# Weight rounding around the Fourier products of the second batch: one pause in place of two

## The chip, the cores and the metric

The kernel runs on one core of a Trainium2 chip. The metric is the device time of one execution in microseconds (us), and the number compared is the median over several runs. A profile is one execution seen by the hardware profiler; its times count from the first instruction. Its engine names are used throughout: PE is TensorE (PEld its weight loads), DVE is VectorE, ACT is ScalarE, POOL is GpSimd and SP is SyncE, which here only issues DMAs.

## The reference

Eight batches of 576 tokens go through chunked attention (8 heads of 64, chunks of 64 tokens), then through a block that adds the real part of a two-dimensional Fourier transform, normalises, and runs a two-layer MLP with a residual:

```python
scores = scale * np.matmul(q_c, k_c.transpose(0, 1, 2, 4, 3))   # in chunks of 64
attn = softmax(scores)                                          # shortened here
x = (attn @ v_c), heads joined: (8, 576, 512)
mixed = np.real(fft(fft(x, axis=1), axis=2))
u = x + mixed
un = (u - mean(u)) / sqrt(var(u) + 1e-6)
out = u + maximum(un @ w_ch1, 0) @ w_ch2      # w_ch1: 512 x 2048, w_ch2: 2048 x 512
```

The two weight matrices come in 64-bit floating point and must be rounded to 32 bits on the chip. All products are in fp32.

## The kernel before, in words

**Groups and tiles.** The tokens are cut into tiles of 128 rows. `groups` are sets of four tiles that pass the MLP together; group 0 is the first batch, group 1 the second, and so on, and the 64 tokens left over in each batch ("rest" tiles) form a group at the end. `mlp(g)` is a Python generator that issues group g's products and yields after each step: 16 steps for the first layer, then 16 for the second (`down_plain`, line L1095, for group 0). So steps 1 to 16 are group 0's first layer and steps 17 to 32 its second; step 17 + m handles row block m. Each engine has its own queue and takes its instructions from it in the order in which the program lists them, and so does SP with the DMAs that it issues. Engines meet only through semaphores.

**Side work.** Beside `mlp(g)` the driver issues the attention and the Fourier transform of the next batch, `side(b)`, also a generator. For batch 1 it has 26 steps: 17 of attention, three empty ones (PAUSE), and six of `fourier(1)`. The driver spreads them over steps 4 to 25. The attention's steps fall so that attention's last step is issued in step 18, the empty ones in steps 19 and 20, and `fourier(1)` begins in step 21.

**`fourier(b)`** (printed below) makes the token transform in two halves: `z_sets(.., 0)` for the first (L669, and the one-row products L679), then the rest and `z_sets(.., 1)` for the second. ScalarE copies results out (L708, L694), VectorE joins them (`z_joined`, L699, L703), ScalarE writes them in transform order to `zr` and `zf` (L720 to L738). Then each of three `mixed` tiles follows (rest tile first, L788 on TensorE): ScalarE copies half of it (L793, L794), VectorE forms both signs (L798, L799) and adds them to x (L805; the mirrored tiles on POOL), then takes mean and variance (L652, L653), whose inverse root ScalarE forms (L656, L657). The mixing tiles use two PSUM buffers in turn. `normed` (L942 on ScalarE) and `turned` (four PE transposes, L347) later make group 1's operand from them: the first of these is issued with step 26 and step 28.

**Rounding.** The weights are cut into 32 pieces of 128x512. `round_weight(i)` issues the head of piece i (two VectorE instructions, L322 and L325, and three on ScalarE, L314, L317, L320) and the tail of piece i - 1 (three on VectorE, L335, L336, L337), which needs the ScalarE results of that piece. After the tail it issues the load of a further piece (L299, on SP). The driver calls it through `round_next`, once or twice a step, unless a side step of this step was marked heavy:

```python
while done < due:
    heavy = next(sides[cur], None) or heavy
    done += 1
...
if not heavy:
    round_next()
    if t <= 2 or t < KF and t % 4 == 0 or t >= KF + 3:      # KF = 16
        round_next()
if n_w > len(pieces) and t >= KF + 7:
    for _ in range(3):
        next(conv2, None)
```

A generator's yielded value belongs to the work issued ahead of that yield. `n_w` counts the roundings; the value 33 is reached when all are issued.

**After the rounding.** `conv2` runs `keep2(i)` for i = 0 to 3: four VectorE subtractions (L1017) that form combined blocks of w_ch2 in `yall` (i even) or `xall` (i odd), one per driver call, then seven stores of 256 KB to the DRAM buffer s2, issued on SP (L1021), then the next i. `conv1` does the same for w_ch1 on POOL (L999, L1003) from step 32 on. They share SP's queue with the loads of q and k (L203) and v (L226) for the coming attention tiles, and with the output stores (L977 and half of L986; the other half of L986 leaves from ACT's queue). For batch 2 and later, VectorE transposes q and k (L366) just before a tile's scores (L398), and a tile's q or k buffer is loaded again right after that.

Of the kernel before, what the change touches and what calls it, by code (L numbers as in the profile page):

```python
# [16 lines left out]
def kernel(  # L17
# [130 lines left out]
    def kind(n):  # L148
        return tiles[n][0]

    def xt(n):
        return xall[:, place[n], 0:DM + 1]
# [494 lines left out]
    def means(ns):  # L647
        st = sm_p.tile([128, 2, 2], FP32, tag="st", bufs=6 + NP, name="st")
        rstd = sm_p.tile([128, 2], FP32, tag="rstd", bufs=6 + NP, name="rstd")
        for j, n in enumerate(ns):  # L650
            bst = sm_p.tile([128, 6], FP32, tag="bst", name="bst")
            nc.vector.bn_stats(bst, xt(n)[:, 1:DM + 1] if kind(n) == HI else xt(n)[:, 0:DM])  # L652
            nc.vector.bn_aggr(st[:, j], bst)  # L653
            sts[n] = st[:, j, 0:1], rstd[:, j:j + 1]
        g = slice(0, len(ns))
        nc.scalar.activation(out=rstd[:, g], in_=st[:, g, 1], func=ACTF.Ln, bias=eps)  # L656
        nc.scalar.activation(out=rstd[:, g], in_=rstd[:, g], func=ACTF.Exp, scale=-0.5)  # L657
# [3 lines left out]
    def z_sets(z, pm, i, turn_, first=False):  # L661


        for s in range(2):
            for q_ in range(4):
                k, r = (q_ // 2 + turn_) % 2, q_ % 2
                T, p = 2 * k + s, slice(32 * q_, 32 * q_ + 32)
                d0_ = T * HQ if i < NM else s * HQ
                nc.tensor.matmul(  # L669
                    out=z[r][k][:, s * NE:(s + 1) * NE], lhsT=pm[i][p, d0_:d0_ + HQ],  # L670
                    rhs=tk[p, NM - 1 - i if i < NM else NM, k],
                    start=first and s == 0, stop=False, skip_group_check=True,
                )

    def mid_products(outs, pm, i):
        p, m0 = (slice(0, 128), DM) if i < NM else (slice(CH, 128), 2 * HQ)
        for g, out_ in enumerate(outs):
            c0, c1 = halves[g % 2]
            nc.tensor.matmul(  # L679
                out=out_[:, 0:c1 - c0], lhsT=pm[i][p, m0 + g // 2:m0 + g // 2 + 1], rhs=tk[p, NM - 1 - i if i < NM else NM, 0, c0:c1],  # L680
                start=False, stop=i == NM, skip_group_check=True,
            )

    def z_space():


        odd = [ps_t.tile([128, 512], FP32, tag="pt", name="z") for _ in range(2)]
        even = ps_a.tile([128, 2, 512], FP32, tag="att", name="more_z")
        zs[1:] = even, odd
        return odd, [even[:, k] for k in range(2)]  # L690

    def z_odd():
        for k in range(2):
            nc.scalar.copy(zs[0][:, 2 * k:2 * k + 2, 1], zs[2][k][:, 0:2 * NE].rearrange("p (t f) -> p t f", t=2))  # L694

    def z_joined():
        even = zs[1][:, :, 0:2 * NE].rearrange("p k (t f) -> p k t f", t=2)
        z4 = zs[0].rearrange("p (k t) r f -> p k t r f", t=2)
        nc.vector.tensor_tensor(out=z4[:, :, :, 0], in0=even, in1=z4[:, :, :, 1], op=ALU.add)  # L699
        for k in range(2):  # L700
            e, o = even[:, k], z4[:, k, :, 1]
            a, b = (e, o) if k == 0 else (o, e)
            nc.vector.tensor_tensor(out=o, in0=a, in1=b, op=ALU.subtract)  # L703

    def z_middle(outs):
        for g, out_ in enumerate(outs):
            c0, c1 = halves[g % 2]
            nc.scalar.copy(middle[:, g // 2, c0:c1], out_[:, 0:c1 - c0])  # L708
# [4 lines left out]
    def z_tile(zf, i):  # L713


        low, high = zs[0][:, :, 0], zs[0][:, :, 1]
        to = zf[:, :, 128 * i:128 * i + 128].rearrange("p t (c r i) -> p t c r i", c=2, r=2)
        if i == 0:
            for c in range(2):
                nc.scalar.copy(to[:, :, c], by_parity(low[:, :, CH * c + CH:CH * c:-1]))  # L720
            return
        n = (2 * CH + CH - NE + 1) // 2
        nc.scalar.copy(to[:, :, 0, :, 0:n], by_parity(high[:, :, NQ - 1 - 3 * CH:NQ - 1 - 3 * CH + 2 * n]))
        nc.scalar.copy(to[:, :, 0, :, n:], by_parity(low[:, :, NE - 1:2 * CH:-1]))
        nc.scalar.copy(to[:, :, 1], by_parity(high[:, :, CH // 2:CH // 2 + CH]))

    def z_rest(h):

        low, high = zs[0][:, :, 0], zs[0][:, :, 1]
        to = zr[:, :, h].rearrange("p t (r i) -> p t r i", r=2)  # L730
        n = CH // 4
        nc.scalar.copy(to[:, :, :, 0:n], by_parity(high[:, :, 2 * n:0:-1]))
        nc.scalar.copy(to[:, :, 1, 0:1], low[:, :, 0:1])
        for t in (0, 2):
            nc.scalar.activation(
                out=to[:, t:t + 2, :, n:], in_=by_parity(high[:, t:t + 2, 0:2 * n]), func=ACTF.Copy, scale=1.0 - t,
            )
        nc.scalar.copy(to[0:1, 2:3, :, n:], by_parity(high[0:1, 2:3, 0:2 * n]))  # L738
# [3 lines left out]
    def fourier(b):  # L742
        h = b % 2
        zf = one_p.tile([128, 4 * NL + 16], FP32, tag="zf", name="zf")
        zf = zf[:, 0:4 * NL].rearrange("p (t f) -> p t f", t=4)
        zs[0] = one_p.tile([128, 8 * NE], FP32, tag="two", name="zs").rearrange("p (t r f) -> p t r f", t=4, r=2)
        pm = [pms.pop((b, i)) for i in range(NM + 1)]


        z = z_space()  # L750
        for i in range(NM + 1):
            z_sets(z, pm, i, 0, i == 0)
        outs = [z[0][0][32 * g:32 * g + 1, 2 * NE:] for g in range(4)]
        for i in range(NM):
            mid_products(outs, pm, i)
        nc.scalar.copy(middle[:, 0, 0:1], outs[0][:, 0:1])
        yield b == 1
        if b == 1:
            yield
        mid_products(outs, pm, NM)  # L760
        for i in range(NM):
            z_sets(z, pm, i, 1)
        z_middle(outs)
        z_odd()
        if b == 1:
            z_joined()
        else:
            yield
            z_joined()
        nc.scalar.copy(zs[0][0:1, 2], middle)  # L770
        if h == 1:
            z_rest(h)
        for i in range(NM):
            z_tile(zf, i)
        if h == 0:
            z_rest(h)
        yield b == 1

        def mixed(i):
            mix = ps_t.tile([128, 512], FP32, tag="pt", name="mix")  # L780
            zt = zr.rearrange("p t h f -> p t (h f)") if i == NM else zf[:, :, 128 * i:128 * (i + 1)]
            for T, (cols, tab) in enumerate((
                (slice(0, HM + 1, 2), ce),
                (slice(1, HM, 2), co),
                (slice(0, DM, 2), cx),
                (slice(HM + 1, DM, 2), so),
            )):
                nc.tensor.matmul(  # L788
                    out=mix[:, cols], lhsT=zt[:, T], rhs=tab,
                    start=(T == 0), stop=(T == 3), skip_group_check=True,  # L790
                )
            y = three_p.tile([128, XW], FP32, tag="y", name="y")
            nc.scalar.copy(y[:, 0:HM + 1], mix[:, 0:HM + 1])  # L793
            nc.scalar.copy(y[:, DM:DM + 1], mix[:, 0:1])  # L794
            return y, mix

        def both(y, mix):
            nc.vector.tensor_tensor(out=y[:, DM - 1:HM:-1], in0=y[:, 1:HM], in1=mix[:, HM + 1:DM], op=ALU.subtract)  # L798
            nc.vector.tensor_tensor(out=y[:, 1:HM], in0=y[:, 1:HM], in1=mix[:, HM + 1:DM], op=ALU.add)  # L799
            return y  # L800

        def added(y, n):
            x, w = xt(n), DM + (kind(n) == HI)
            eng = nc.gpsimd if kind(n) == HI else nc.vector
            eng.tensor_tensor(out=x[:, 0:w], in0=y[:, 0:w], in1=x[:, 0:w], op=ALU.add)  # L805

        for i in ((NM,) if h == 1 else ()) + tuple(range(NM)):
            y = both(*mixed(i))
            ns = [rests[b // 2]] if i == NM else [at[LO, b, i], at[HI, b, i]]
            for n in ns:  # L810
                added(y, n)
            means(ns)
            yield
# [426 lines left out]
    with tc.manual_schedule():  # L1240
# [48 lines left out]
        def side(b):  # L1289
            yield from attention(b)  # L1290
            for _ in range(PAUSE if b == 1 else PAUSE - 1):
                yield
            yield from fourier(b)
# [107 lines left out]
```

## Time and profile before

| What | Value |
|---|---|
| Median of 5 runs | 1091.36 us (1090.13 to 1094.23) |
| The profiled execution's own time | 1091.36 us |
| Its span, first to last instruction | 1089.6 us |
| Granted TensorE clock, mean over the span | 0.994 |
| DMA traffic | 192.65 MB, mean 177 GB/s |
| Instructions | 19740 |

The span lies 1.8 us under the execution's own time, and that execution is at the median. The page's first part gives each engine's busy time and share; its second part cuts the span into 40 slices of 27.2 us. Further answers of the trace are named by what they list: the timeline (instructions of an engine in order of time, with the idle time before one in brackets and what ended it), the waits (who waited for whom in total, times, and the longest), the chain of waits (followed back from the last instruction) and the table by stretches (busy time of PE, PEld, DVE, ACT and POOL, then the granted TensorE clock, the busy share of the DMA engines and their GB/s).

### The profile page before, as it was taken

To read this page: it belongs to the slowest core of one execution; us is meant where nothing else is said; L and a number is where in the kernel's file an instruction comes from. 1 tells how busy PE (TensorE), PEld (TensorE's weight loads), DVE (VectorE), ACT (ScalarE), POOL (GpSimd) and SP (SyncE) were. 2 spreads that over 40 slices of the span, in tenths; PEclk is the share of its full clock that TensorE was granted. 3 is DMA by queue.
4 is the path that set the end of the run, shared out by engine and by line. 5 is a ranking of instruction groups with operands and counts; after the bars stand their busy time and mean duration, and the time that the engine had idled before them with its cause. 6 is when DMAs were issued, how large, how long until landed. Compare 5 with 4: busy or idle time off the path is not lost.

```text
span 1089.6 us, 19740 instructions
## 1 busy us (share of the span) xinstructions
PE 1058.9 (97%) x7410; PEld 841.3 (77%) x7410; DVE 591.1 (54%) x1287; ACT 309.6 (28%) x730; POOL 308.1 (28%) x459
## 2 busy tenths in 40 slices
PE   8999998889999999999999999999999999999998
PEld 6645454335888888888888888888888888888887
DVE  4899979234456555574456555745664534323411
ACT  4788463111202231223023312331134103101300
POOL 4301001356413441163306240535152401220140
PEclk9999999989999999999999999999999999999999
DMA  8776535688556826794568356864653355446232
GB/s 167 227 209 177 154 107 173 193 273 281 197 183 191 246 97 186 209 264 133 169 203 248 106 179 178 253 171 155 192 191 102 140 183 174 125 153 212 78 116 78
DMA packets 147948, 192.65 MB, mean 177 GB/s; under 512 B 66284, under 2 KB 104172, under 8 KB 140686
## 3 DMA queue, kind: packets, MB, share of 16 engines
q1 hardware_dynamic: 144204, 187.98, 56.5%
q10 hardware_dynamic: 3330, 2.76, 1.0%
q8 instruction: 59, 0.97, 0.4%
q0 software_dynamic: 320, 0.66, 0.3%
q14 instruction: 35, 0.29, 0.1%
HBM read 167.22 MB, written 24.12 MB: 176 GB/s over the span
## 4 chain that ended last, share of the span: by engine, by line
PE 82%; DMA 5%; DVE 5%; SPq 3%; ACT 3%; issue 1%; POOL 0%; DVEq 0%; ACTq 0%; POOLq 0%
PE pb L1190 20%; PE pa L1141 17%; PE pa L1190 15%; PE pb L1141 12%; PE up L1074 4%; PE dn L1095 3%; PE pt L347 2%; PE z L669 2%; PE mix L788 2%; PE xp L448 1%; PE sc L398 1%; PE up L1054 1%; DMA v<-in_v_dram 1%; SPq L216 1%; DMA wb<-s 1%
## 5 line engine op out<-in xcount | busy, mean ns | idle before, releaser
L1141 PE MATMUL pa<-unT,wa 128*128 128x256 f32 x672 | 159.9, 381 | 1.2 <-DVE wa L1149 1.2
L1141 PEld LDWEIGHTS pa<-unT,wa 128*128 128x128 f32 x672 | 126.2, 190 | 19.1 <-DVE wa L1149 1.7
L1042 POOL TENSOR_TENSOR h<-h 128x256 f32<-128x256 f32 x64 | 55.0, 866 | 230.5 <-DVE wb L1040 137.5
L1190 PE MATMUL pa<-wb,h 128*128 128x256 f32 x512 | 115.7, 380 | 0.0
L1190 PE MATMUL pb<-wb,h 128*128 128x256 f32 x512 | 114.9, 379 | 0.0
L1141 PE MATMUL pb<-wa 128*128 128x256 f32 x448 | 106.6, 381 | 0.0
L1190 PEld LDWEIGHTS pa<-wb,h 128*128 128x128 f32 x512 | 96.0, 190 | 13.0
L1190 PEld LDWEIGHTS pb<-wb,h 128*128 128x128 f32 x512 | 96.3, 190 | 12.6
L1141 PEld LDWEIGHTS pb<-wa 128*128 128x128 f32 x448 | 84.3, 190 | 11.5
L1147 DVE TENSOR_TENSOR wa<-pb,wa 128x256 f32<-128x256 f32 x56 | 23.8, 425 | 69.1 <-ACT wa L1146 69.1
L1074 PE MATMUL up<-unT,wa 128*128 128x512 f32 x128 | 60.8, 629 | 0.0
L1095 PE MATMUL dn<-wb,h 128*128 128x512 f32 x128 | 57.5, 597 | 2.6 <-ACT h L1065 2.6
L505 POOL COPY xall<-xall 1x512 f32<-1x512 f32 x28 | 17.3, 619 | 149.7 <-DVE xall L465 120.4
L1190 PE MATMUL pb<-wb,yall 128*128 128x256 f32 x256 | 58.2, 381 | 0.0
L1190 PE MATMUL pb<-wb 128*128 128x256 f32 x256 | 57.7, 379 | 0.0
L1190 PE MATMUL pa<-wb,yall 128*128 128x256 f32 x256 | 57.6, 379 | 0.0
L1146 ACT COPY wa<-pa 128x256 f32<-128x256 f32 x56 | 20.9, 372 | 123.5 <-PE pa L1141 87.4
L1141 PE MATMUL pa<-wa 128*128 128x256 f32 x224 | 53.9, 383 | 0.0
L1141 PE MATMUL pb<-unT,wa 128*128 128x256 f32 x224 | 52.9, 379 | 0.0
L1190 PEld LDWEIGHTS pa<-wb,yall 128*128 128x128 f32 x256 | 48.0, 190 | 6.1
L1190 PEld LDWEIGHTS pb<-wb,yall 128*128 128x128 f32 x256 | 47.7, 190 | 6.3
L1190 PEld LDWEIGHTS pb<-wb 128*128 128x128 f32 x256 | 47.6, 190 | 5.9
(265 smaller groups left out, 1756.1 us busy)
## 6 DMA issues: line engine op xcount, KB each, us to landing
wb<-s SPq DMA_DIRECT2D x56, 1024.0 KB
wa<-s SPq DMA_DIRECT2D x196, 256.0 KB
xall<-in_moe_w_ch_dram SPq DMA_DIRECT2D x22, 512.0 KB
q<-in_q_dram SPq DMA_DIRECT2D x96, 112.0 KB
k<-in_k_dram SPq DMA_DIRECT2D x96, 112.0 KB
v<-in_v_dram SPq DMA_DIRECT2D x124, 64.0 KB
yall<-in_moe_w_ch_dram SPq DMA_DIRECT2D x10, 512.0 KB
s<-wb SPq DMA_DIRECT2D x20, 256.0 KB
```

The lines of the kernel that those rows point to most:

```text
L216: eng.dma_start(out=t[p0:p0 + np_], in_=src[b, :, c * CH:c * CH + np_, :].rearrange("h p d -> p h d"))
L347: nc.tensor.transpose(pt[:, j, :], src(j), ident)
L505: nc.gpsimd.tensor_copy(to, from_)
L669: nc.tensor.matmul(out=z[r][k][:, s * NE:(s + 1) * NE], lhsT=pm[i][p, d0_:d0_ + HQ], rhs=tk[p, NM - 1 - i if i < NM else NM, k], start=fir ...
L788: nc.tensor.matmul(out=mix[:, cols], lhsT=zt[:, T], rhs=tab, start=(T == 0), stop=(T == 3), skip_group_check=True,)
L1042: nc.gpsimd.tensor_tensor(out=h1[:, m, hi], in0=h1[:, m, lo], in1=h1[:, m, hi], op=ALU.subtract)
L1074: nc.tensor.matmul(out=up, lhsT=w1[:, kk, m * 128:(m + 1) * 128], rhs=unT[:, kk], start=(kk == 0), stop=(kk == KD - 1),)
L1095: nc.tensor.matmul(out=dn, lhsT=h1[:, m, s * 128:(s + 1) * 128], rhs=w2[:, m, :], start=(m == 0), stop=(m == KF - 1),)
L1141: nc.tensor.matmul(out=dst, lhsT=w[:, kk, r], rhs=rhs[o][:, kk], start=(o in (0, 1) and kk == 0), stop=(kk == 1), skip_group_check=True,)
L1146: nc.scalar.copy(a, dst)
L1147: nc.vector.tensor_tensor(out=b, in0=pbs[r][:, 0], in1=a, op=ALU.add)
L1190: nc.tensor.matmul(out=dst, lhsT=lhs[:, m], rhs=w[:, m], start=(o in (0, 2) and m == 0), stop=(m == HF - 1), skip_group_check=True,)
```

## The change

In `fourier(1)` the first half of the products is no longer marked heavy, the empty step between the halves is, and the second half no longer is. For the other batches the marks were false and stay so. The instructions are the same; only where roundings are issued among them changes.

```diff
         nc.scalar.copy(middle[:, 0, 0:1], outs[0][:, 0:1])
-        yield b == 1
+        yield
         if b == 1:
-            yield
+            yield True
         mid_products(outs, pm, NM)
...
         if h == 0:
             z_rest(h)
-        yield b == 1
+        yield
```

Roundings per driver step, and the value that `n_w` has after the step:

| Step | Side work of batch 1 | Before | After |
|---|---|---|---|
| 20 | two empty steps | 2 (28) | 2 (28) |
| 21 | first half of the products | none (28) | 2 (30) |
| 22 | empty | 2 (30) | none (30) |
| 23 | second half, copies to zr and zf | none (30) | 2 (32) |
| 24 | mixing, rest tile | 2 (32) | 1, tail alone (33) |
| 25 | mixing, two tiles | 1, tail alone (33) | none (33) |

With n_w at 33 a step earlier, `conv2` starts in step 24 instead of 25 and is three calls ahead in each later step.

## The prediction, made before the changed kernel was run

> **What bounds the kernel now.** I read the page first: its engine table and the slices.
>
> ```profile
> PE 1058.9 (97%) x7410; PEld 841.3 (77%) x7410; DVE 591.1 (54%) x1287; ACT 309.6 (28%) x730; POOL 308.1 (28%) x459
> ```
>
> TensorE is busy for 1058.9 of 1089.6 us; 30.7 us are idle. An edit that moves no matrix product can pay only in these, or in time at half clock. The list of waits, for TensorE over the whole span, says where they end:
>
> ```profile
> PE sc L398 <- DVE rd L461: 8.6, 1, 8.6
> PE pt L347 <- ACT un L942: 3.6, 3, 2.0
> PE pt L347 <- ACT ex L424: 2.7, 2, 2.0
> ...
> PE pa L1141 <- DVE wa L1149: 1.2, 2, 0.6
> ```
>
> The largest is one wait. In the timeline (TensorE) it stands at 223.36 us, after two of 2 us:
>
> ```profile
> 171.85 0.66 PE L347 MATMUL pt<-ident,un 128*128 128x128 f32 x4 [2.04 <-ACT un L942]
> 208.36 0.78 PE L347 MATMUL pt<-ident,ex 128*128 128x128 f32 x4 [2.00 <-ACT ex L424]
> 208.93 5.21 PE L1074 MATMUL up<-unT,wa 128*128 128x512 f32 x8
> 223.36 1.13 PE L398 MATMUL sc<-kT,qT 64*64 64x64 f32 x32 [8.60 <-DVE rd L461]
> ```
>
> From 223.4 to the end TensorE waits only 1.2 us more (the row L1141), so a shift of 223.4 shifts the end. What ends the 8.6 us? The wait names L461, but the timeline of VectorE, whose queue is in order, has L461 behind a transpose that waits for a DMA, and the chain of waits goes on into the queue of SP:
>
> ```profile
> 222.22 1.09 DVE L366 STREAM_TRANSPOSE kT<-k 128x512 f32<-128x512 f32 x1 [13.54 <-DMA k<-in_k_dram]
> ```
>
> ```profile
> 205.60 0.62 SPq L977
> 206.22 0.06 issue
> 206.28 8.80 DMA out_dram<-o
> 215.08 0.02 issue
> 215.09 0.34 SPq L203
> ...
> 216.98 5.11 DMA k<-in_k_dram
> ```
>
> So a load of k, issued behind the first output stores, sets TensorE's time at 223.4. The stores' data was ready long before: VectorE's L1108 wrote it from 189.49 to 191.96. They left at 205.60 because SP still had the copies that keep2 writes to s2 (L1021) in front. Why SP was late is in its own waits and timeline:
>
> ```profile
> SPq L1021 <- DMA out_dram<-o: 4.1, 1, 4.1
> ```
>
> ```profile
> 189.51 5.29 SPq L1021 DMA_DIRECT2D s<-yall  x3
> ```
>
> One store of s2 out of yall waited 4.1 us for an output store that ACT's queue had issued at 190.80. The two share no data; I read it as a completion counter that the queues use in turn. After it (194.48) SP issued 18 more DMAs up to 205.60: 0.62 us each. Last, the table by stretches: DMA (the last two columns) stands idle from 152 to 172, just before the copies start.
>
> ```profile
> 152.00:156.00 4.00, 4.00 (x16) 2.27 (x15) 2.10 (x4) 1.76 (x8) 0.00 (x0) 1.00 0.00 0
> 168.00:172.00 4.00, 1.97 (x6) 0.66 (x5) 3.68 (x8) 1.88 (x7) 1.02 (x1) 1.00 0.00 0
> 208.00:212.00 4.00, 3.64 (x8) 1.93 (x9) 0.68 (x1) 1.38 (x3) 2.22 (x2) 0.59 0.23 59
> ```
>
> **The change, part by part.** *The first half moves nothing.* By the counts of the driver, step 21 issues the first half of the products and step 22 nothing. The two roundings of step 22 go to step 21. No other VectorE work lies between, and ACT has only L756 there, ahead of them in both. They keep 141.50 to 147.05, and the last two weight loads that they issue on SP (143.49, 146.44) keep their place: zero, as no queue's order changes.
>
> *The second half moves two roundings past the rest tile's mixing,* from step 24 to the end of step 23. On VectorE they fill a hole: L703 ends at 150.38, L798 waits until 153.79 (3.4 us). Two roundings take 5.2 (156.26 to 161.5). But their six ACT instructions now stand ahead of L793 on ACT. ACT is done with zf at 153.35; the six take about 3.9 back to back (0.53, 0.74 and 0.65 a piece, from their starts at 156.81, 157.33 and 158.07). L798 therefore starts at 157.7, not 153.79, and the rest tile ends at 157.7 + 2.55 = 160.25. No load is left for them to issue; the loads that they read were issued by 146.44, and two such loads that VectorE did wait for had landed 3.5 us after theirs (135.33 to 138.89, 140.89 to 144.44): about 150, ahead of the use at 153.0.
>
> *What follows.* The counter n_w reaches 33 in step 24, not 25, so keep2 starts a step earlier. VectorE in step 24: the last piece's tail, 1.9 (169.88 to 171.78), and three of keep2's subtractions, 1.93 (171.78 to 173.71). The next tile's L798 starts at 164.1 instead of 161.64: 2.5 later, and so do the means and L942. TensorE first meets a mixing tile that waits for its PSUM buffer (L799 of the rest tile ends at 158.85, it ran at 157.42: 1.4), then un at 174.35, a wait of 3.1 in place of 2.04. The 0.67 us wait for ex at 177.04 is swallowed. TensorE is then 2.5 - 0.67 = 1.8 behind.
>
> *The clock.* After the wait of 2.0 at 208.36, the eight matmuls took 5.21 us against 3.60, with a granted clock of 0.59 in 208 to 212: it lost 1.6. After 2.04 at 171.85 nothing was lost. A wait of 3.1 lies above both, so I take 1.7 as its price; bounds 0 and 1.7. TensorE is then 3.5 late near 190.
> [...]
>
> *The DMAs of keep2.* Its first copies can leave at 163 to 167, in the idle stretch; the second seven at 174 to 178, ahead of the q loads rather than behind (181.00 to 185.34); the third at 181 to 185 instead of 188.80 to 196.37. SP is seven DMAs ahead in its order. Two bounds for the first output store:
> - Not held by the counter: q loads at 179.4, then in turn third copies, k, v, fourth copies, q to about 195.8, that is 9.8 earlier than 205.60.
> - Held as before: release at 194.45 + 3.5, less some 1.4 because fewer copies crowd that output store (it took 3.6 us): 196.5. With 18 - 7 = 11 still to issue, less 2 because TensorE is later while SP is not: 9 x 0.62 = 5.6, hence 202.1, 3.5 earlier.
>
> I take the second, being nearest to a row that was seen. The k load lands 16.5 after that store, as now (205.60 to 222.1): 218.6, and sc starts at 219.9 instead of 223.37. TensorE is there at 214.77 + 3.5 - 2.0 (the wait at 208.36 goes, the copies it stood on being done) - 1.6 (its half clock) = 214.7. The long wait becomes 5.2 and the half clock after it stays. Sum: -3.5 us on the profiled execution, whose own time of 1091.36 is also the median: 1087.9.
>
> **The rivals.**
> - *SP is not held.* k lands at 212.3, before TensorE wants it. The gain is then 223.37 - 214.7 = 8.7, and the half clock after the long wait goes (24 matmuls took 12.94; at 3.43 for eight they take 10.3, and sc 1.13 against 0.65): 2.9 to 3.1. About 1079.8. For it: 20 us of idle DMA are put to use. Against: the counter's hold is there now.
> - *Gain eaten.* The hold falls with 12 to 15 issues left: 203.9 to 205.8. The time is then 1089.7 to 1091.6. Also here: a k load set by something that does not move.
> - *Slower.* One mechanism: the shared counter. TensorE's lateness delays ACT's output stores, and SP is held on them with all 18 issues left: 196.5 + 11.1 = 207.6, 2.0 late, and the end with it: 1093.4; with a longer landing some 1 to 2 more. It decides from (205.6 - 196.5) / 0.62 = 15 issues left upward.
>
> **How the numbers follow.** Forecast (held, 9 left, 1086 to 1089.5): 0.42. Not held: 0.20. Eaten: 0.18. Slower: 0.20. About 0.2% (2.2 us) is what a measurement of this kernel can tell from no change. Faster by more takes the first two cases: 0.62; same 0.18; slower 0.20. The range reaches down to the unheld case, 1079.0, and up to the slower one, 1093.5; it leaves out deeper gains and a longer hold. The likeliest case's own range is 1086 to 1089.5.
>
> **What would show it.** VectorE without the hole at 150.4 to 153.8, L322 there; L798 of the rest tile near 157.7; the PSUM wait at a mixing tile and the wait for un near 3 us at 174, followed by half clock; s2 copies in the DMA table at 163 to 167; the first output store of SP at 202; the wait at 208.36 gone and the long one near 5 us. I am wrong if the store leaves at or after 205, if the six ACT instructions do not delay L793, or if TensorE finds a new wait behind 223.

## The result, and the profile after

The changed kernel takes 1089.68 us (median of 35 runs, 1086.95 to 1094.19), the kernel before 1091.86 in the 61 runs beside it: ratio 0.9979, 95% interval [0.9972, 0.9987], a gain of 2.2 us. The forecast was 1087.9 with a range of 1079.0 to 1093.5. The profiled execution took 1087.15 us (span 1085.4), 4.2 less than the one of before, and the medians show 2.2 of that.

The page's engine table of the changed kernel, busy time and share:

```profile
PE 1057.5 (97%) x7410; PEld 841.1 (77%) x7410; DVE 592.7 (55%) x1287; ACT 309.6 (29%) x730; POOL 307.9 (28%) x459
```

TensorE's idle time fell from 30.7 to 27.9 us. Its list of waits, changed kernel (total, times, longest):

```profile
PE sc L398 <- DVE rd L461: 6.9, 1, 6.9
PE pt L347 <- ACT un L942: 4.6, 3, 3.0
...
PE mix L788 <- DVE y L799: 1.1, 1, 1.1
```

The long wait at the scores is 1.7 shorter, the wait for un 1.0 longer, the PSUM wait at the mixing tile is new, and ex (L424) has left the list. VectorE's timeline around the rest tile, changed kernel (start, duration, and the idle time before in brackets):

```profile
149.95 0.42 DVE L322 TENSOR_SCALAR wb<-xall 128x512 uint32<-128x512 uint32 x1
...
155.81 0.69 DVE L337 TENSOR_TENSOR wb<-wb,power 128x512 f32<-128x512 f32 x1
157.28 0.42 DVE L798 TENSOR_TENSOR y<-y,mix 128x255 f32<-128x255 f32 x1 [0.78 <-PE mix L788]
...
161.65 0.68 DVE L1017 TENSOR_TENSOR yall<-wb 128x512 f32<-128x512 f32 x1
...
163.58 0.41 DVE L798 TENSOR_TENSOR y<-y,mix 128x255 f32<-128x255 f32 x1
```

The hole is filled from 149.95 on; the rest tile starts at 157.28 instead of 153.79. The releaser is given as PE, but the ACT timeline shows what was last:

```profile
153.05 0.62 ACT L314 ACTIVATE wb<-wb 128x512 f32<-128x512 uint32 x1
...
156.21 0.72 ACT L320 ACTIVATE power<-power,top 128x512 uint32<-128x512 uint32 x1
156.84 0.35 ACT L793 COPY y<-mix 128x257 f32<-128x257 f32 x1
157.09 0.16 ACT L794 COPY y<-mix 128x1 f32<-128x1 f32 x1
```

ACT's six rounding instructions, from 153.05 on, stand ahead of L793, and L794 ends at 157.25, just before L798 starts. TensorE's timeline at the places named in the prediction, and the table by stretches after the wait for un (the value after the five engines is the granted clock), both of the changed kernel:

```profile
173.78 1.10 PE L347 MATMUL pt<-ident,un 128*128 128x128 f32 x4 [3.01 <-ACT un L942]
174.67 4.88 PE L1095 MATMUL dn<-wb,h 128*128 128x512 f32 x8
...
208.92 0.60 PE L347 MATMUL pt<-ident,ex 128*128 128x128 f32 x4
209.36 3.60 PE L1074 MATMUL up<-unT,wa 128*128 128x512 f32 x8
...
220.51 1.13 PE L398 MATMUL sc<-kT,qT 64*64 64x64 f32 x32 [6.92 <-DVE rd L461]
```

```profile
172.00:176.00 4.00, 2.22 (x6) 1.57 (x7) 3.93 (x7) 3.72 (x12) 0.00 (x0) 0.73 0.70 233
176.00:180.00 4.00, 4.00 (x13) 1.86 (x12) 3.97 (x7) 1.31 (x2) 0.48 (x2) 0.84 0.86 304
```

After 3.01 us of idle the clock was 0.73 and 0.84 (0.50 in 174 to 177), and the next eight matmuls took 4.88 us instead of 3.60. At 208.92 wait and half clock are both gone (1.00 in 208 to 212). Last, SP in the changed kernel: its largest wait for a DMA between 125 and 260 us, the two places in its timeline, and what VectorE waits for:

```profile
SPq L226 <- DMA out_dram<-o: 5.6, 1, 5.6
```

```profile
188.16 8.17 SPq L226 DMA_DIRECT2D v<-in_v_dram  x4
...
202.95 1.20 SPq L977 DMA_DIRECT2D out_dram<-o  x2
```

```profile
219.37 1.08 DVE L366 STREAM_TRANSPOSE kT<-k 128x512 f32<-128x512 f32 x1 [12.69 <-DMA k<-in_k_dram]
```

SP is still held, now at a load of v, until 195.05. The first output store leaves at 202.95 (205.60 before), VectorE's transpose of k starts at 219.37 (222.22), the scores at 220.51 (223.36): 2.85 us earlier. Of the profiled execution's gain, 0.7 more lies in the 24 matmuls behind the wait (12.27 us instead of 12.94) and 0.6 in the waits at L1141 (0.6 instead of 1.2).

### The profile page after: what moved, and what is told of

The parts are those of the page before. It is cut to its first block, busy times and chain, and to the rows that moved or that the text cites. A ratio compares the mean times of both kernels' runs of the same rounds, so it can differ in the third digit from the quotient of the medians.

```text
span 1085.4 us, 19741 instructions
## 1 busy us (share of the span) xinstructions
PE 1057.5 (97%) x7410; PEld 841.1 (77%) x7410; DVE 592.7 (55%) x1287; ACT 309.6 (29%) x730; POOL 307.9 (28%) x459
## 4 chain that ended last, share of the span: by engine, by line
PE 88%; DVE 5%; ACT 3%; DMA 3%; issue 1%; SPq 0%; POOL 0%; ACTq 0%; DVEq 0%; POOLq 0%
PE pb L1190 20%; PE pa L1141 18%; PE pa L1190 15%; PE pb L1141 13%; PE up L1074 4%; PE dn L1095 4%; PE pt L347 3%; PE mix L788 2%; PE z L669 2%; PE sc L398 2%; PE xp L448 2%; PE up L1054 1%; DMA v<-in_v_dram 1%; PE idle L1270 1%; DVE power L336 1%; DMA out_dram<-o 1%
## 5 line engine op out<-in xcount | busy, mean ns | idle before, releaser
L1141 PE MATMUL pa<-unT,wa 128*128 128x256 f32 x672 | 159.9, 381 | 0.6 <-DVE wa L1149 0.6
L1141 PEld LDWEIGHTS pa<-unT,wa 128*128 128x128 f32 x672 | 126.2, 190 | 18.3 <-DVE wa L1149 0.8
L1141 PE MATMUL pb<-wa 128*128 128x256 f32 x448 | 106.6, 381 | 0.0
L1141 PEld LDWEIGHTS pb<-wa 128*128 128x128 f32 x448 | 84.3, 190 | 11.5
L1074 PE MATMUL up<-unT,wa 128*128 128x512 f32 x128 | 58.5, 610 | 0.0
L1141 PE MATMUL pa<-wa 128*128 128x256 f32 x224 | 53.9, 383 | 0.0
L1141 PE MATMUL pb<-unT,wa 128*128 128x256 f32 x224 | 52.9, 379 | 0.0
```

Source lines behind the costliest of these rows:

```text
L1074: nc.tensor.matmul(out=up, lhsT=w1[:, kk, m * 128:(m + 1) * 128], rhs=unT[:, kk], start=(kk == 0), stop=(kk == KD - 1),)
L1141: nc.tensor.matmul(out=dst, lhsT=w[:, kk, r], rhs=rhs[o][:, kk], start=(o in (0, 1) and kk == 0), stop=(kk == 1), skip_group_check=True,)
```

## The experiments

Ratios are against runs of the kernel before in the same batch. Times within a trace shift from one execution to another: the first store to s2, which no edit moves, leaves at 146.82 before, at 146.68 after, and between 146.61 and 149.67 in the others. Where two kernels' times are set against each other below, the difference in that start is taken off, or a length within one trace is used. Theories keep the letters they have in the quoted expectations. "The hold" is the stretch in which SP stands at one DMA until an output store of ACT's queue has landed; issues left at its end are counted with the held DMA.

The first half of the edit moves nothing: in the program built with it alone, every engine has the same instructions in the same order as before, and in that with the second half alone the same as after.

**Which part of the change pays: the moved roundings or the earlier copies?** Two kernels, one with each part.

```diff
 # e1_copies_late, the changed kernel: keep2 from step 25, as before
-if n_w > len(pieces) and t >= KF + 7:
+if n_w > len(pieces) and t >= KF + 9:
 # e2_copies_early, the kernel before: keep2 from step 24
-if n_w > len(pieces) and t >= KF + 7:
+if t >= KF + 8:
```

> The changed kernel, but keep2 starts in step 25 as it did before the change; the roundings stay where the change put them. Theory A (the gain comes from keep2's seven copies standing earlier in SP's queue): the gain goes, SP's order is that of before, the first output store leaves near 205 and the long wait of the scores (L398) is back at 8 to 9 us: 1091 to 1092.5. Theory B (the gain comes from the roundings filling VectorE's hole at 150.4 to 153.8): the gain stays, about 1089.7.

> The kernel before, its roundings where they were, but keep2 starts in step 24 as in the changed kernel. Theory A: the gain is there without the moved roundings, as SP's order is that of the changed kernel; VectorE's three subtractions still stand ahead of the next mixing tile (1.9 us), so TensorE waits about 4 us for un near 174 and then loses 1 to 1.7 us to half clock: 1088 to 1090. Theory B: no gain, 1091.5 to 1093.

e1: 1090.11 us, ratio 0.9978 [0.9965, 0.9991]. e2: 1089.98, ratio 0.9975 [0.9959, 0.9992]. Each part alone gives the whole gain. Theory A, that the earlier copies are what pays, fell with e1, and theory B, that the filled hole is, with e2. The two come there by different ways. In e1 TensorE waits 1.09 for un instead of 2.04, and 0.64 for ex (at 206.95) instead of 0.67 and 2.00, ACT's first output store is issued 1.2 us earlier, and SP is held for 2.8 instead of 4.1. In e2 the wait for un is 3.77 with the clock at 0.65 and 0.50 in 172 to 180; ACT's store is 2.9 later, but only 14 issues are left to SP at the release, not 19.

**Is the hold the limit?** Group 0's four stores that leave from ACT's queue are given to POOL's.

```diff
 # e3_pool_stores, the changed kernel
-eng = nc.scalar if r else nc.sync
+eng = (nc.gpsimd if n in groups[0] else nc.scalar) if r else nc.sync
```

> The changed kernel, with the four output stores of group 0 that left from ACT's queue issued from POOL instead. Theory A with the shared completion counter as the hold: the wait of the v load on an output store (5.6 us) goes, the first output store of SP leaves near 197.5 instead of 202.95, the load of k lands near 214, TensorE's long wait shrinks to 0 to 2 us and the half clock after it goes: 1081 to 1085. Rival C (the hold is the DMA traffic itself, not the counter): SP stands still about as long, 1089 to 1090. POOL issues four DMAs more, which may delay its own conv1 work by some us.

1082.9 us, ratio 0.9908 [0.9888, 0.9929]. SP's timeline, e3:

```profile
179.85 1.88 SPq L203 DMA_DIRECT2D q<-in_q_dram  x4
...
188.36 2.65 SPq L226 DMA_DIRECT2D v<-in_v_dram  x4
...
198.21 1.20 SPq L977 DMA_DIRECT2D out_dram<-o  x2
```

The four loads of v take 2.65 us, not 8.17: the hold is gone with ACT's stores. The instructions' own records name what SP had waited for: the load held in the changed kernel waits for the completion counter of the store that ACT issued at 192.74 (both DMAs name counter 105), and that store landed at 195.04, 0.01 before the load was issued. The scores wait 1.26 us at 215.93, and the clock stays at 1.00 after it.

**Why does k land 16 us behind the first store?** Group 0's mirrored low-tile stores (L977) are written as two stores of 32 rows each, in unmirrored row order, so these rows of the output stand in the wrong places.

```diff
 # e4_forward_rows, the changed kernel, group 0 only
-                nc.sync.dma_start(out=to, in_=o[r0:r0 + CH])
+                if n in groups[0]:
+                    for r in range(2):
+                        nc.sync.dma_start(
+                            out=out[b, t0 + 1 + r:t0 + CH + 1:2, :], in_=o[r0 + ODD * r:r0 + ODD * r + ODD]
+                        )
+                else:
+                    nc.sync.dma_start(out=to, in_=o[r0:r0 + CH])
```

> The changed kernel; group 0's four stores of the low tiles, each one DMA with rows in mirrored order and a slowest dimension of two, are written as two DMAs each of 32 rows in forward order (so these rows of the output stand in the wrong order). Theory D (the load of k lands late because these four stores run on few DMA engines and k's packets queue behind them): SP issues four DMAs more (2.4 us) but k lands 2 to 3 us after its own issue, near 214.5 instead of 219.25; the long wait shrinks from 6.9 to about 2 us: 1083 to 1086. Rival (k is late only because SP issues it late): 1089.5 to 1092.

1081.87 us, ratio 0.9895 [0.9874, 0.9917], though SP is held as before (4.7 us, first store at 204.64). In the changed kernel the four mirrored stores land at 208.4, 211.2, 214.2 and 217.7, one after another, and the k loads behind them at 218.3 to 219.25, 7 to 8 us after their issue. The records of those four loads say why: each counts 16 steps to its landing, 14 of them are in by 213.65 to 214.95, and the last two come 3.3 to 4.7 us later, when the stores are through. Each mirrored store shows one early step and two late ones. In e4 each half lands 1.6 to 3.0 us after its issue and k lands by 214.05, 2.4 after its last issue. TensorE's timeline, e4:

```profile
215.36 0.69 PE L398 MATMUL sc<-kT,qT 64*64 64x64 f32 x32 [0.25 <-DVE rd L461]
```

So two things lie in a row between SP and the scores: the hold, and mirrored stores that land 2.6 to 3.5 us apart (before and after). Taking away either makes nearly the whole wait vanish. e4 changes the number of stores, their shape and the order of rows at once; which of these frees k was not separated by a run.

**Does a later start of the copies hurt?**

```diff
 # e5_copies_later, the changed kernel: keep2 from step 26
-if n_w > len(pieces) and t >= KF + 7:
+if n_w > len(pieces) and t >= KF + 10:
```

> The changed kernel with its moved roundings, but keep2 starts in step 26, one step later than before the change. Asked after both halves by themselves (roundings moved alone; keep2 early alone) gave the whole gain. Theory A2 (both gain by one thing: keep2's copies leave earlier in time, by order or because VectorE gets to them sooner, so SP is let go earlier): the copies leave later than before here, the first output store of SP leaves at 205 or after on before's time axis, and the gain is gone: 1091.5 to 1094. Theory B (VectorE's filled hole pays by itself, TensorE waiting less near 172 to 177): 1089 to 1090.5.

1087.68 us, ratio 0.9956 [0.9943, 0.9969]: better than the change itself, against the theory. The wait for un is 1.11, no half clock follows (1.00 in 172 to 180), q and k go ahead of the second copies, and SP is held at a later place, for 2.6 us with 13 issues left. That an earlier start of keep2 is a gain for its own sake is refuted. What matters is what SP still has to issue when it is released: e5's first output store leaves 4.0 us earlier than that of the kernel before, e1's 2.0 and e2's 1.1.

**Can the k load simply go first?** Group 0's stores are issued after the k loads of the next tile, in step 33; alone in the kernel before (e7), in the changed one (e6), and in the changed one with keep2 from step 25 (e8).

```diff
 # e6_loads_first, e7_before_loads_first, e8_both
-                    store(n, o)
+                    late.append((n, o))
...
+                if t == begin[1] + 1:
+                    for n, o in late:
+                        store(n, o)
```

> The changed kernel; group 0's output stores are issued in step 33 behind the k loads instead of in step 32 ahead of them. Theory D (k's packets stand behind four stores that run on few DMA engines): the k loads leave near 203 and land near 207, before TensorE wants them at 214, and the long wait with its half clock goes: 1081 to 1084. Rival (the bound is SP's pace or the next load behind the stores): the q and v loads behind the stores take over and 1085 to 1090 results.

> The kernel before with the same reordering. Theory D: k lands near 209, TensorE is there at 214.8 as before, so the 8.6 us wait and its half clock go; the 2 us wait at 208 and its half clock stay: 1080 to 1083. The change is then worth nothing or costs 0 to 2 us, as its gain was all in that wait. Rival (the change saves time of its own): 1 to 3 us slower than the changed kernel with the reordering.

> The reordering, the moved roundings, and keep2 from step 25 as before the change: TensorE then waits 1.1 us for un near 172 in place of 2.0 (before) or 3.0 (changed), without half clock at 174 to 178. If the long wait is gone, this is worth 1.5 to 3.5 us against the changed kernel with the reordering: 1078.5 to 1081.5. If the load of k is still what is waited for, no difference.

e6: 1090.65, ratio 0.9985 [0.9969, 1.0001]. e7: 1092.91, 1.0009 [0.9993, 1.0025]. e8: 1091.77, 1.0002 [0.9988, 1.0016]. None beats the change, and all three missed their expectations of 1078.5 to 1084. k lands at 210.64 in e6 and the wait near 220 is gone, but SP is held for 7.8 us and the next tile meets the wait. TensorE's timeline, e6:

```profile
238.86 1.13 PE L398 MATMUL sc<-kT,qT 64*64 64x64 f32 x32 [8.17 <-DVE rd L461]
```

The next loads of q now stand behind the same stores. The order of the two is thus not the bound. That the time of the stores in SP's path is, fits e3 and e4; in e6 the longer hold stands beside it, and no run parts the two.

**What is the change worth without the hold?** POOL stores in the kernel before (e9), and with the moved roundings alone (e12: e1 and e3 together).

> The kernel before, with group 0's output stores taken off ACT's queue and issued from POOL (as in e3_pool_stores, which had the change and was 9.6 us faster than before). Question: is the change worth anything once SP is not held? Theory C (the hold only hides the change's seven DMAs of advance): the hold of 4.1 us at the s2 store goes, SP issues its 19 DMAs from 190.4 at 0.6 us each, the first output store leaves near 202, k lands 16.5 later at 218.4, scores start near 219.7 and the long wait is about 5 us; gain against before 3.7 us, ratio 0.9966, so about 6 us slower than e3_pool_stores. Rival (the change acts on nothing but the hold): as fast as e3_pool_stores, ratio 0.991.

> The changed kernel with keep2 from step 25, as before the change (e1_copies_late), and with group 0's ACT-queue output stores issued from POOL, so that SP is not held. Only the moved roundings are left of the change. Theory F (without the hold, SP's place in its queue decides: 0.61 to 0.64 us an issue from the first q load, 37 issues up to the first output store in before's order and 30 in the changed one): SP starts these 1.6 us earlier than in before, as in e1, issues 37, and the store leaves at about 178.1 + 37 x 0.63 = 201.4; k 16.4 us later at 217.8, scores at 219.1, a long wait of 5 to 6 us: about 1088 to 1089, ratio 0.996 to 0.997, close to e9_before_pool (1090.45) and 5 to 6 us behind e3_pool_stores. Rival (the moved roundings alone are worth the whole gain, as they were beside the hold): near e3_pool_stores, ratio 0.991.

e9: 1090.45 us, ratio 0.9983 [0.9973, 0.9993]. e12: 1087.48, ratio 0.9951 [0.9936, 0.9966]. SP's timeline, e9 and then e12:

```profile
181.50 1.76 SPq L203 DMA_DIRECT2D q<-in_q_dram  x4
...
194.32 3.10 SPq L226 DMA_DIRECT2D v<-in_v_dram  x4
...
205.09 1.22 SPq L977 DMA_DIRECT2D out_dram<-o  x2
```

```profile
179.82 1.76 SPq L203 DMA_DIRECT2D q<-in_q_dram  x4
...
202.61 1.21 SPq L977 DMA_DIRECT2D out_dram<-o  x2
```

e9's gain is about half of the 3.7 us expected, e12 a little better than its 1088 to 1089. In none of the three does SP stand for a store of ACT's queue, and from the first q load to the first output store it needs 23.6 us for 37 DMAs (e9), 22.8 for 37 (e12) and 18.4 for 30 (e3): 0.64, 0.62 and 0.61 each. The rival, that the roundings alone are worth all of it, fell; so did, with e9, the one that the change acts on nothing but the hold. The four corners:

| Ratio to before | ACT's stores as they were | Stores from POOL |
|---|---|---|
| Neither part | 1 | 0.9983 (e9) |
| Moved roundings | 0.9978 (e1) | 0.9951 (e12) |
| Earlier copies | 0.9975 (e2) | not run |
| Both: the change | 0.9979 | 0.9908 (e3) |

Beside the hold either part is worth some 2.5 us and both together no more. Without it the second part still pays on top of the first: about 3.5 us (0.0032) for the roundings, which start SP's run of issues 1.6 us earlier, and then 4.7 (0.0043) for the earlier copies, which take seven issues out of SP's run of 37. The three ratios come from different batches, and their intervals leave each of these steps uncertain by some 2 us or more. What the copies alone are worth without the hold is the empty corner, so that the two simply add is not shown.

**Do the edits that helped add up?** e10 is e5 and e3 together; in e11 group 0's mirrored stores go to POOL as well.

```diff
 # e11_later_pool_all, beside the lines of e3 and e5
-nc.sync.dma_start(out=to, in_=o[r0:r0 + CH])
+(nc.gpsimd if n in groups[0] else nc.sync).dma_start(out=to, in_=o[r0:r0 + CH])
```

> The changed kernel with both of the edits that helped: keep2 from step 26 (e5_copies_later, -4.9 us against before) and group 0's output stores from POOL instead of ACT (e3_pool_stores, -10 us). Theory C: both act on the same path, SP's order up to the first output store. In e5 13 issues were left at a hold of 2.6 us, so without it the store leaves at 196.5 - 2.6 + 13 x 0.61 = 201.8, k lands near 218.3, on an axis that starts 2.4 us later than e3's: scores 1.3 us later than in e3, less 1.1 to 3 us of un wait and half clock that TensorE no longer has: 1082 to 1086. Rival: the gains add, since e5's lies in TensorE's wait for un and e3's in the hold: about 1079.

> As e10_later_pool, and the four mirrored stores of group 0's low tiles go to POOL's queue as well; SP keeps half of the high tiles' stores. Theory E (k's load is late because it stands behind mirrored stores that land 2.6 us after one another): k lands about 10 us earlier, no wait at the scores near 220 and no half clock after it; 1079 to 1081, or 1.5 to 3 us under e10. Rival (as e6_loads_first): the mirrored stores keep their few DMA engines as long from POOL's queue, the counters or POOL's own work pass the wait on to the next tile's loads, and nothing is gained on e10.

e10: 1086.33 us, ratio 0.9942 [0.9929, 0.9954]; e11: 1083.92, 0.9921 [0.9906, 0.9937]. e10 shows them not adding: keep2 from step 26 puts the seven copies back into SP's run (37 issues, 23.6 us), and without a hold that is what counts, so the order that was better beside the hold is worse without it. e10 came 0.3 us above its expected 1082 to 1086, and the 1079 of its rival is far off. e11 is 2.4 under e10, as expected between them, but 3 us above the forecast of 1079 to 1081. TensorE's timeline, e11, and a line of SP's:

```profile
210.24 0.66 PE L347 MATMUL pt<-ident,ex 128*128 128x128 f32 x4 [1.64 <-ACT ex L424]
...
230.91 0.69 PE L398 MATMUL sc<-kT,qT 64*64 64x64 f32 x32 [0.49 <-DVE rd L461]
```

```profile
194.33 7.11 SPq L203 DMA_DIRECT2D q<-in_q_dram  x4
```

The long wait is gone, a shorter one is left at 210. SP's run of 37 is 28.5 us here (178.30 to 206.75), 4.8 longer than in e10: it is slow at four loads of q while POOL issues its eight stores, and the profile names no wait of over 0.3 us there. The stores of the copies behind these loads come late too, and before the wait at 210 VectorE waits 5.83 us for one of them. That may be why e11 is no faster than e3; what slows the four issues stays open. Of the kernels that compute everything, e3 has the lowest ratio, about 1% under before: the change with four stores moved to POOL. By the intervals e11 is not apart from it. Low-tile stores that keep the mirrored order but spread as e4's do were not tried; neither were the earlier copies alone with POOL's stores.

## Why the prediction was right

**First half: nothing moves.** Right, by the order of instructions on each engine.

**Second half: L798 at 157.7, the rest tile's end at 160.25.** Measured 157.28 and 159.75, and the six ACT instructions are the cause, as forecast: 3.9 us were put on them, and they ran from 153.05 to 156.93.

**What follows.** The PSUM wait was 1.05 (forecast 1.4; the 158.85 in its working is too late, since L798 at 157.7 and the 0.88 us from there to the end of L799 give 158.58), the next tile's L798 at 163.58 (164.1), the wait for un 3.01 (3.1), the wait for ex gone.

**The clock.** Forecast 1.7 us lost. Measured 1.29 on the eight matmuls (from 172.34 to 175.77 before, from 174.67 to 179.39 after) and 0.40 on the four transposes ahead of them: 1.7. TensorE's next layer starts at 193.46 instead of 190.73, and its first mixing tile had been 0.3 earlier: 3.1 late, forecast 3.5. Here 3.01 us of idle (granted clock 0.73 and 0.84 in the two stretches after) and the 2.00 at 208.36 before (0.59) were followed by a lower clock, 1.09 in e1 and 2.04 at 171.85 before (1.00 in 172 to 180 in both) were not. What separates 2.00 from 2.04 no run shows; the forecast took the upper of its bounds, 0 and 1.7, and that one came.

**The DMAs.** The step that was mis-sized is the number of issues left at the release. I took 18 - 7 - 2 = 9 behind the held one; it was 12 (13 with it, 19 with it before). The two taken off for TensorE's lateness have no ground in a run: in e1, which has before's order, 19 with it are left again, in e2, which has the changed one, 14. The release was early by 1.45 us (195.05 against 196.5), since ACT's store was less late (192.74 instead of 190.80, 1.9 where 3.5 was taken); it landed in 2.30 us instead of 3.62, 1.3 less where 1.4 was taken. Two lines of VectorE show the term that was missed, the first of the kernel before, the second of the changed one:

```profile
189.49 2.47 DVE L1108 TENSOR_TENSOR o<-dn,xall 128x512 f32<-128x512 f32 x4
```

```profile
191.16 0.69 DVE L1108 TENSOR_TENSOR o<-dn,xall 128x512 f32<-128x512 f32 x1 [1.29 <-PE dn L1095]
```

Before, L1108, which writes the store's data, came straight behind a copy on VectorE (L1017) and did not wait for TensorE; in the changed kernel it does, so only part of TensorE's lateness reached the store. The error in the issues and that in the release go against each other, and that the store left at 202.95, so near 202.1, is in part luck. k landed at 219.25 (forecast 218.6), 16.3 behind it (16.5).

**The sum.** Scores at 220.51, forecast 219.9; TensorE was there at 213.59 (214.7), so the long wait was 6.9 and not 5.2, and the half clock behind it stayed (0.50 in 219 to 225), as said. 2.85 us instead of 3.5 on the path, 2.2 in the medians. The mechanism was the forecast's: SP advances in its order, and a hold takes part of that back. By issues left and by the median, though, the outcome lies at the edge of the rival "gain eaten" (12 to 15 left, 1089.7 to 1091.6), and the store's 202.95 lies halfway between the forecast's 202.1 and that rival's 203.9. 1089.68 lies 0.2 over the likeliest case's own range of 1086 to 1089.5, and the gain lies at the bound of 2.2 between faster and same.

**The rivals.** "SP is not held" was priced at 1079.8; with the hold removed, e3 gave 1082.9, and what separated it from the changed kernel was that hold, not anything in the Fourier step. "Slower" needed 15 issues left or more behind the held one; with ACT's store delayed by 2.9 us e2 had 13 behind it and still gained. What I had not asked is what the change would be worth in another order of stores: 2.2 us beside the hold, some 8 without it (e9 against e3).

## What to carry to other kernels

When a wait sits on a DMA, follow its queue back to the first stretch in which the queue issues without a stop; count the DMAs in it and multiply by the time of one issue, then look for a place where the queue stands still. An edit that takes DMAs out of such a stretch pays only as far as the standstill lets it, and two edits that advance the same queue need not add up: here each gave alone what both gave together. And look at where the transfers ahead in the queue land, not only at when they are issued.

## What the runs showed of the hardware

- A DMA of SP waited 4.1, 5.6, 2.8, 4.2, 4.7, 2.6 and 7.8 us (before, after, e1, e2, e4, e5, e6) until an output store of ACT's queue had landed with which it shares no data; with that store on POOL's queue it did not (e3, e9, e10, e12). In the instructions' records of before and after, the DMAs of SP and ACT name eight completion counters in turn (101 and 103 to 109), and POOL's name others (110 to 117). The held DMA and ACT's store name the same one: 107 before, complete at 194.42, the DMA issued at 194.48; 105 after, complete at 195.04, issued at 195.05.
- SP's issues took 0.61 to 0.64 us each over runs of 30 or 37 DMAs of 64 to 256 KB in which it was not held (e3, e9, e10, e12), and 0.77 in e11.
- The mirrored 64-row stores (128 KB) landed 2.6 to 3.5 us apart (before and after), one after another, and their counters rose in 3 steps, those of the loads and copies around them in 16. While one of them alone was under way, the DMA engines' busy share was 0.13, two of 16, at 49 GB/s (after, 208.5 to 209.5; before, 215.5 to 216). Of the 16 steps of each k load behind them, the last two came 3.3 to 4.7 us after the other 14 (after). In e4, written as two stores with 32 rows outermost, the halves landed 1.6 to 3.0 us after their issue, several at a time; the 32-row stores that go beside the mirrored ones (L986) rose in 16 steps before and after. What sets the number of steps, and of engines, no run shows.
